# A third of w2 loaded by four 32-row transfers that only eight of the sixteen DMA engines carry

## The chip, the cores and the metric

The kernel runs on one core of a Trainium2 chip. The metric is the device time of one execution in microseconds. All runs quoted are in the fast state, except the single run of e4, whose state is unknown; the profile is of one such execution, and its span is about 2 us shorter than the time. In the profile, DVE is VectorE, PE is TensorE (PEld its weight loads), ACT is ScalarE, and SP issues loads. "Engine" without such a name means one of the sixteen DMA engines.

## The reference, cut to what matters

```python
# x (4, 1, 640), 32 heads of 192, K and V caches (4, 32, 8192, 192), window W = 2048, all bf16
xn = layernorm(x)
q = (xn @ wq), by head
p = softmax(q . k_window * 192 ** -0.5);  o = p . v_window
attention = o @ wo                                   # wo (6144, 640)
h = silu(xn @ w1) * (xn @ w3)                        # w1, w3 (640, 1536)
ffn = h @ w2                                         # w2 (1536, 640)
return x + attention + ffn
```

It is a decode step: four tokens against 201 MB of K and V. Everything is read once, 223 MB in all.

## The kernel before

K and V of a head are one transfer of 3 MB each, 128 partitions by 24,576 bytes; two K tiles and three V tiles are in memory at a time. DVE multiplies K by q, TensorE adds over the head size, a chain of small instructions makes the softmax, TensorE takes P times V. All loads but a first small one of x come from one queue, SP's, in program order. The feed-forward part is spread between the heads; its last weight, w2, comes at the very end.

```python
def ffn_h():                       # h, and its 32x32 transposes, so that 128 of the 1536 rows lie on 128 partitions
    nc.vector.tensor_tensor(out=hb[:].rearrange("p c r -> p r c"),
                            in0=ffn.pop("ps")[:].rearrange("p (r c) -> p r c", c=FC),
                            in1=sT[:].rearrange("p (r c) -> p r c", c=FC), op=ALU.mult)
    nc.vector.transpose(out=hT[:].rearrange("p c r -> p (c r)"), in_=hb[:].rearrange("p c r -> p (c r)"))

w2_v = B_w2.rearrange("(p c) n -> p c n", c=FC)      # FC = 12 columns of rows on 128 partitions
W2C = [0, FC - 4, FC - 2, FC]                        # three pieces: 8, 2 and 2 columns

def w2_load(i):
    if i == 0:
        ffn["w2"] = fpool.tile([P, FC, D], BF16, tag="w", name="w2")
    c0, c1 = W2C[i:i + 2]
    nc.sync.dma_start(out=ffn["w2"][:, c0:c1, :].rearrange("p c n -> p (c n)"),
                      in_=w2_v[:, c0:c1, :].rearrange("p c n -> p (c n)"))

def ffn_out(i):
    for c in range(*W2C[i:i + 2]):
        acc_add(hT[:, c, 0:B], ffn["w2"][:, c, :], last=(c == FC - 1))
# ... (cut)
for h in range(H - 2, H):                            # the order of the last loads, behind the last K tile
    add(NU - 6, 0, load_v, h, 1 + (h == H - 1))
add(NU - 6, 0, w2_load, 0)
add(NU - 6, 0, wo_load, NG - 2)
add(NU - 6, 0, wo_load, NG - 1)
add(NU - 6, 0, w2_load, 1)
add(NU - 6, 0, w2_load, 2)
add(e - 1, 8, ffn_out, 0)
add(e - 1, 8, ge_proj, NG - 2, 0, RPP)               # ge_proj: the attention output times wo
add(e, 6, ge_proj, NG - 1, 0, RPP)
add(e, 7, ffn_out, 1)
add(e, 7, ffn_out, 2)
```

Of the kernel before, what the change touches and what calls it, by code (L numbers as in the profile page):

```python
# [12 lines left out]
ALU = mybir.AluOpType  # L13
# [5 lines left out]
def kernel(  # L19
# [20 lines left out]
    nc = tc.nc  # L40
# [6 lines left out]
    FC = F // P  # L47
# [8 lines left out]
    CT = 32  # L56
    QW = HG * Dh
    RPP = QW // P
    NU = H * GQ
# [54 lines left out]
    for k0 in range(0, KC, 2):  # L114
        n = min(2, KC - k0)
        wt = vpool.tile([P, 2, H * Dh], BF16, tag="vt")
        nc.sync.dma_start(out=wt[:, 0:n, :].rearrange("p k n -> p (k n)"),
                          in_=wq_v[:, k0:k0 + n, :].rearrange("p k n -> p (k n)"))
# [83 lines left out]
    def acc_add(lhsT, rhs, last=False):  # L202
        for i in range(2):
            acc_half(i, lhsT, rhs, last=last)
# [120 lines left out]
    sT = const.tile([P, FW], FP32, name="sT")  # L325
    hb = const.tile([P, FC, CT], BF16, name="hb")
    hT = const.tile([P, FC, CT], BF16, name="hT")
    ffn = {}
# [14 lines left out]
        nc.scalar.activation(out=sT[:], in_=ffn.pop("ps")[:], func=ACTF.Silu)  # L343

    def ffn_h():
        nc.vector.tensor_tensor(out=hb[:].rearrange("p c r -> p r c"),
                                in0=ffn.pop("ps")[:].rearrange("p (r c) -> p r c", c=FC),
                                in1=sT[:].rearrange("p (r c) -> p r c", c=FC), op=ALU.mult)
        nc.vector.transpose(out=hT[:].rearrange("p c r -> p (c r)"), in_=hb[:].rearrange("p c r -> p (c r)"))

    w2_v = B_w2.rearrange("(p c) n -> p c n", c=FC)
    W2C = [0, FC - 4, FC - 2, FC]

    def w2_load(i):
        if i == 0:
            ffn["w2"] = fpool.tile([P, FC, D], BF16, tag="w", name="w2")
        c0, c1 = W2C[i:i + 2]
        nc.sync.dma_start(out=ffn["w2"][:, c0:c1, :].rearrange("p c n -> p (c n)"),
                          in_=w2_v[:, c0:c1, :].rearrange("p c n -> p (c n)"))
# [4 lines that stand above are left out]
# [3 lines left out]
    def add(slot, phase, fn, *args):  # L367
        sched[slot].append((phase, len(sched[slot]), fn, args))
# [31 lines left out]
    e = ends[H - 1][1] + 1  # L400
    for hg in range(NG - 2):
        a = ((hg + 1) * HG - 1) * GQ + L + 3
# [7 lines left out]
    add(f + 8, 0, ffn_load, "w3", B_w3)  # L410
    add(f + 15, 7, ffn_in, "w3")
    add(f + 15, 9, ffn_h)
    add(8, 0, x_load)
    add(16, 6, x_add, 0)
    add(17, 6, x_add, 1)


    for h in range(H - 2, H):
        add(NU - 6, 0, load_v, h, 1 + (h == H - 1))
    add(NU - 6, 0, w2_load, 0)  # L420
    add(NU - 6, 0, wo_load, NG - 2)
    add(NU - 6, 0, wo_load, NG - 1)
    add(NU - 6, 0, w2_load, 1)
    add(NU - 6, 0, w2_load, 2)
    add(e - 1, 8, ffn_out, 0)
    add(e - 1, 8, ge_proj, NG - 2, 0, RPP)
    add(e, 6, ge_proj, NG - 1, 0, RPP)
    add(e, 7, ffn_out, 1)
    add(e, 7, ffn_out, 2)

    for s in sorted(sched):
        for phase, _, fn, args in sorted(sched[s], key=lambda e: (e[0], e[1])):
# [38 lines left out]
```

## Time and profile before

| | before |
|---|---|
| time, median of 3 runs | 529.59 us (529.48 to 531.6) |
| span of the profiled run | 527.6 us |
| moved | 223.31 MB, 423 GB/s |
| DVE, PE busy | 65%, 67% |
| last K tile landed, by its sixteen completion records | 498.62 us |
| last piece of w2 landed | 523.85 us |
| last instruction (copy of the result) starts | 524.62 us |

The lines of this profile stand in the prediction below. Two more things of the trace are used throughout. *Completion records*: a 128-partition transfer leaves sixteen, the small reload of x four, each of the change's new transfers eight (with fewer than sixteen the trace has one more at the issue, which is not counted here). They are taken as one from each engine that carried the transfer, as it is done, so the spread of the sixteen tells how far apart the engines run. *Packet records*: size, start and duration of every packet, without the engine's number. Undisturbed, a packet of 24,576 bytes takes 0.912 us, of 12,288 bytes 0.460, of 7,680 bytes 0.291 and of 2,560 bytes 0.102; in the kernels with 5,120-byte rows, an undisturbed row takes 0.196.

### The profile page before, as it was taken

The page shows a single profiled execution, that of the slowest core. Times are in us where ns is not written, and L with a number is a line of the kernel's source. Part 1 is how long each engine was busy: PE and PEld are TensorE (multiplying, and loading weights), DVE is VectorE, ACT ScalarE, POOL GpSimd, SP SyncE. Part 2 cuts the span into 40 slices and gives each one's busy share as a digit, 9 for nine tenths or more (in the row PEclk, how much of TensorE's full clock was granted, in tenths as well). Part 3 has the DMA queues.
Part 4 walks back from the last instruction along what each step waited for, and adds up shares of the span by engine and source line. Part 5 has one row for each costly group of instructions (what it writes and reads, how often), then busy time and mean ns, then how long its engine had stood idle before and what let it go on. Part 6 is the DMA issues. An engine that isn't in the chain of part 4 may idle for free.

```text
span 527.6 us, 5428 instructions
## 1 busy us (share of the span) xinstructions
PE 353.5 (67%) x2306; PEld 142.6 (27%) x2307; DVE 345.6 (65%) x435; ACT 45.6 (9%) x143; POOL 1.1 (0%) x8
## 2 busy tenths in 40 slices
PE   2865886765657476577637866577566777675686
PEld 0322332322212232223212322223222332232233
DVE  3179775776458567686637876577657867677661
ACT  2111000100211000000000000000000000000010
POOL 0000000000000000000000000000000000000000
PEclk9889887899878989789997998789997988799788
DMA  8999999999999999999999999999999999999994
GB/s 358 434 430 415 420 439 434 430 434 419 439 438 427 432 427 437 429 434 428 432 432 432 432 427 435 432 432 430 432 430 432 432 430 434 429 435 427 438 419 203
DMA packets 11719, 223.31 MB, mean 423 GB/s; under 512 B 1312, under 2 KB 1328, under 8 KB 2608
## 3 DMA queue, kind: packets, MB, share of 16 engines
q1 hardware_dynamic: 11680, 222.97, 98.6%
q8 instruction: 18, 0.29, 0.2%
q14 instruction: 5, 0.04, 0.0%
q10 hardware_dynamic: 16, 0.01, 0.0%
HBM read 222.96 MB, written 0.01 MB: 423 GB/s over the span
## 4 chain that ended last, share of the span: by engine, by line
DMA 57%; DVE 22%; PE 18%; ACT 2%; issue 1%; SPq 0%
DMA kt<-in_A_k_cache_dram 54%; DVE pr L219 15%; PE ps L230 9%; PE po L307 4%; DVE sc L238 3%; DMA wt<-in_A_wq_dram 3%; PE qps L179 2%; PE o_ps L282 2%; DVE z L274 1%; ACT ex L266 1%; PE mt L260 1%; DVE oT L315 1%; DVE og L312 0%; PE acc L200 0%; ACT L266 0%
## 5 line engine op out<-in xcount | busy, mean ns | idle before, releaser
L230 PE MATMUL ps<-pr,idb 128*128 128x512 bf16 x768 | 208.5, 412 | 152.3 <-DVE pr L219 152.3
L219 DVE TENSOR_TENSOR pr<-kt,qbc 128x3072 bf16<-128x3072 bf16 x128 | 223.5, 1746 | 113.9 <-DMA kt<-in_A_k_cache_dram 113.9
L230 PEld LDWEIGHTS <-idb 128*128 128x128 bf16 x768 | 74.4, 102 | 258.7 <-issue 200.1
L238 DVE TENSOR_REDUCE sc<-ps 128x16 f32<-128x512 f32 x128 | 87.2, 681 | 2.0 <-PE ps L230 2.0
L282 PE MATMUL o_ps<-vt,z 128*8 128x384 bf16 x1024 | 60.6, 373 | 2.7 <-DMA vt<-in_A_v_cache_dram 2.7
L307 PE MATMUL po<-o_sb,sel_w 128*32 128x192 f32 x128 | 49.1, 517 | 1.1 <-ACT o_sb L289 1.1
L282 PEld LDWEIGHTS <-z 128*8 128x8 bf16 x1024 | 26.2, 94 | 32.8 <-issue 22.8
L289 ACT COPY o_sb<-o_ps 128x384 f32<-128x384 f32 x32 | 15.3, 479 | 189.7 <-PE o_ps L282 189.7
L274 DVE TENSOR_TENSOR z<-ex,mask_b 128x256 bf16<-128x256 bf16 x32 | 13.5, 422 | 22.0 <-ACT ex L266 22.0
L263 ACT COPY negm<-mt 128x1 f32<-128x1 f32 x32 | 5.1, 159 | 259.0 <-PE mt L260 259.0
L307 PEld LDWEIGHTS po<-o_sb,sel_w 128*32 128x32 f32 x128 | 13.6, 128 | 26.8 <-issue 25.0
L179 PE MATMUL qps<-wt,xnT 128*128 128x512 bf16 x59 | 17.2, 456 | 4.8 <-DMA wt<-in_A_wq_dram 4.7
L185 DVE CAST qbc<-qps 128x512 bf16<-128x512 f32 x6 | 3.8, 684 | 18.7 <-PE qps L179 18.7
L260 PEld LDWEIGHTS mt<-ones_ff,gneg 1*128 1x128 f32 x64 | 9.5, 186 | 13.8 <-issue 11.7
L252 DVE TENSOR_REDUCE gmax<-mt 1x4 f32<-1x128 f32 x32 | 8.8, 275 | 6.6 <-PE mt L247 6.6
L260 PE MATMUL mt<-ones_ff,gneg 1*128 1x1 f32 x64 | 12.2, 258 | 0.0
L247 PE MATMUL mt<-idf,lmax 128*1 128x128 f32 x32 | 10.6, 330 | 1.1 <-DVE lmax L242 1.1
L266 ACT ACTIVATE ex<-sc,negm 128x64 bf16<-128x64 f32 x32 | 11.1, 348 | 1.0
L179 PEld LDWEIGHTS <-xnT 128*128 128x128 bf16 x60 | 6.7, 112 | 14.8 <-issue 9.7
L200 PE MATMUL acc<-wo_t,oT 128*4 128x320 bf16 x96 | 9.2, 298 | 0.4 <-DVE oT L315 0.4
L294 PEld LDWEIGHTS po<-rsum,tot_w 128*32 128x32 f32 x64 | 4.6, 110 | 14.1 <-issue 12.5
L242 DVE TENSOR_REDUCE lmax<-sc 128x1 f32<-128x64 f32 x32 | 7.0, 220 | 1.1
(52 smaller groups left out, 64.2 us busy)
## 6 DMA issues: line engine op xcount, KB each, us to landing
kt<-in_A_k_cache_dram SPq DMA_DIRECT2D x32, 3072.0 KB, 19.0
vt<-in_A_v_cache_dram SPq DMA_DIRECT2D x31, 3072.0 KB, 26.1
wo_t<-in_A_wo_dram SPq DMA_DIRECT2D x8, 960.0 KB, 20.5
wt<-in_A_wq_dram SPq DMA_DIRECT2D x2, 3072.0 KB, 13.3
w<-in_B_w_dram SPq DMA_DIRECT2D x2, 1920.0 KB, 27.1
vt<-in_A_v_cache_dram SPq DMA_DIRECT2D x2, 1536.0 KB, 31.2
wt<-in_A_wq_dram SPq DMA_DIRECT2D x1, 1536.0 KB
w<-in_B_w_dram SPq DMA_DIRECT2D x1, 1280.0 KB, 33.6
```

Source lines behind the costliest of these rows:

```text
L179: nc.tensor.matmul(qp[:], lhsT=xnT[:, kc].rearrange("p a b -> p (a b)"), rhs=wq_rows[kc][:, (c0 + i) * QC:(c0 + i + 1) * QC], start=(kc == ...
L200: nc.tensor.matmul(acc[i * CT:i * CT + B, :], lhsT=lhsT, rhs=rhs[:, i * N0:(i + 1) * N0], start=first, stop=last)
L219: nc.vector.tensor_tensor(out=pr[:], in0=kts[h][:, g * JQ:(g + 1) * JQ, :], in1=qbc[:, h * Dh:(h + 1) * Dh].unsqueeze(1).to_broadcast([P, ...
L230: nc.tensor.matmul(ps[:], lhsT=idb[:], rhs=pr[:, :, kk * DD:(kk + 1) * DD], start=(kk == 0), stop=(kk == NK - 1))
L238: nc.vector.tensor_reduce(out=scs[h][:, g * JQ:(g + 1) * JQ], in_=pss.pop(u)[:], axis=AX.X, op=ALU.add)
L247: nc.tensor.transpose(out=mt[0:1, 0:P], in_=chs[h][0][:], identity=idf[:])
L260: nc.tensor.matmul(mt[:, P:P + 1], lhsT=gneg[:].rearrange("o p b -> o (p b)"), rhs=ones_ff[0:1, 0:1], start=True, stop=True)
L266: nc.scalar.activation(out=ex[:], in_=scs.pop(h)[:], func=ACTF.Exp, bias=negm[:, 0:1], scale=SCALE, accum_out=rsum[:])
L274: nc.vector.tensor_tensor(out=z[:], in0=ex[:].unsqueeze(2).to_broadcast([P, NJ, B]), in1=mask_b[:].unsqueeze(1).to_broadcast([P, NJ, B]), ...
L282: nc.tensor.matmul(o_ps[c * CT:c * CT + 2 * B, :], lhsT=z[:, 2 * jj:2 * jj + 2, :], rhs=vt[:, 2 * jj:2 * jj + 2, :], start=(jj < 4), stop= ...
L289: nc.scalar.copy(out=o_sb[:], in_=o_ps[:])
L307: nc.tensor.matmul(po[sl, 0:Dh], lhsT=sel_w[:, par].rearrange("p a b -> p (a b)"), rhs=o_sb[:, par * Dh:(par + 1) * Dh].rearrange("p (r i) ...
```

## The change

The last transfers end on one half of the engines 2 to 3 us before the other half (the last piece of w2: seven records at 519.27 to 520.03 us, eight at 521.77 to 522.58, one at 523.85). The change gives a third of w2 (columns 0 to 3 of 12, 655 kB) to eight engines alone, so that the others have less to do. To confine it to eight, the 32 rows are named in HBM as 8 by 4 (each of the four new transfers left eight records), and h is permuted to match by four small multiplies. The third is also moved ahead of the last two V tiles, right behind the last K tile.

```diff
--- before.py
+++ after.py
@@ -343,17 +343,27 @@
         nc.scalar.activation(out=sT[:], in_=ffn.pop("ps")[:], func=ACTF.Silu)
 
     def ffn_h():
-        nc.vector.tensor_tensor(out=hb[:].rearrange("p c r -> p r c"),
-                                in0=ffn.pop("ps")[:].rearrange("p (r c) -> p r c", c=FC),
-                                in1=sT[:].rearrange("p (r c) -> p r c", c=FC), op=ALU.mult)
+        ps = ffn.pop("ps")
+        nc.vector.tensor_tensor(out=hb[:, WB:FC, :].rearrange("p c r -> p r c"),
+                                in0=ps[:].rearrange("p (r c) -> p r c", c=FC)[:, :, WB:FC],
+                                in1=sT[:].rearrange("p (r c) -> p r c", c=FC)[:, :, WB:FC], op=ALU.mult)
+        for a in range(CT // 8):
+            nc.vector.tensor_tensor(out=hb[:, 0:WB, a:CT:CT // 8].rearrange("p c r -> p r c"),
+                                    in0=ps[:].rearrange("p (r c) -> p r c", c=FC)[:, a * 8:a * 8 + 8, 0:WB],
+                                    in1=sT[:].rearrange("p (r c) -> p r c", c=FC)[:, a * 8:a * 8 + 8, 0:WB], op=ALU.mult)
         nc.vector.transpose(out=hT[:].rearrange("p c r -> p (c r)"), in_=hb[:].rearrange("p c r -> p (c r)"))
 
     w2_v = B_w2.rearrange("(p c) n -> p c n", c=FC)
-    W2C = [0, FC - 4, FC - 2, FC]
+    WB = 4
+    W2C = [0, WB, FC - 4, FC - 2, FC]
 
     def w2_load(i):
         if i == 0:
             ffn["w2"] = fpool.tile([P, FC, D], BF16, tag="w", name="w2")
+            for w in range(HG):
+                nc.sync.dma_start(out=ffn["w2"][w * CT:(w + 1) * CT, 0:WB, :].rearrange("p c n -> p (c n)"),
+                                  in_=w2_v[w * CT:(w + 1) * CT, 0:WB, :].rearrange("(a e) c n -> e a (c n)", e=8))
+            return
         c0, c1 = W2C[i:i + 2]
         nc.sync.dma_start(out=ffn["w2"][:, c0:c1, :].rearrange("p c n -> p (c n)"),
                           in_=w2_v[:, c0:c1, :].rearrange("p c n -> p (c n)"))
@@ -415,18 +425,20 @@
     add(17, 6, x_add, 1)
 
 
+    add(NU - 6, 0, w2_load, 0)
     for h in range(H - 2, H):
         add(NU - 6, 0, load_v, h, 1 + (h == H - 1))
-    add(NU - 6, 0, w2_load, 0)
+    add(NU - 6, 0, w2_load, 1)
     add(NU - 6, 0, wo_load, NG - 2)
     add(NU - 6, 0, wo_load, NG - 1)
-    add(NU - 6, 0, w2_load, 1)
     add(NU - 6, 0, w2_load, 2)
+    add(NU - 6, 0, w2_load, 3)
     add(e - 1, 8, ffn_out, 0)
+    add(e - 1, 8, ffn_out, 1)
     add(e - 1, 8, ge_proj, NG - 2, 0, RPP)
     add(e, 6, ge_proj, NG - 1, 0, RPP)
-    add(e, 7, ffn_out, 1)
     add(e, 7, ffn_out, 2)
+    add(e, 7, ffn_out, 3)
 
     for s in sorted(sched):
         for phase, _, fn, args in sorted(sched[s], key=lambda e: (e[0], e[1])):
```

## The prediction

In the prediction, and in what was expected of the runs, the engines that carry the new transfers are called the *lower* eight, the rest the *upper* eight. The trace does not number engines; that the four of x are among the lower, and that those are the ones that run ahead, were my assumptions. *Port conflict* is my name for a loss that I supposed where lower engines write partitions 64 to 127 while upper ones have packets in flight. That two engines would then get half the speed each was my estimate, from no trace.

> **What bounds the kernel now.** I read the page first (engine shares, the 40 slices, the queues, the chain by engine), then the chain in order of time for the last 48 us, then the timeline of that stretch, then a table of one-microsecond windows for the last transfers, and at last the completion records of each transfer (one per DMA engine, sixteen per transfer).
>
> The page: the DMA row of the 40 slices, the chain by engine, and the queues.
>
> ```profile
> DMA  8999999999999999999999999999999999999994
> ...
> DMA 57%; DVE 22%; PE 18%; ACT 2%; issue 1%; SPq 0%
> ...
> q1 hardware_dynamic: 11680, 222.97, 98.6%
> q8 instruction: 18, 0.29, 0.2%
> q14 instruction: 5, 0.04, 0.0%
> ```
>
> The transfers run at their full rate until the last slice: 38 of 40 slices show 9. The kernel streams 223 MB, and the chain is DMA, with short pieces of DVE and PE between. Besides the data queue there are 18 packets of instructions on q8 (16,384 bytes each) and a few on q14. They look like nothing; the argument needs them below.
>
> The chain in order of time, end of the kernel (start us, us, what):
>
> ```profile
> 479.88 18.75 DMA kt<-in_A_k_cache_dram
> 498.62 0.02 issue
> 498.64 1.77 DVE pr L219
> ...
> 513.89 2.69 PE o_ps L282 x32
> ...
> 520.03 0.49 ACT o_sb L289
> ...
> 522.16 0.43 DVE og L312
> 522.62 0.39 DVE oT L315
> 523.01 0.04 issue
> 523.05 1.54 PE acc L200 x20
> 524.59 0.02 issue
> 524.62 0.48 DVE res L437
> ```
>
> The last transfer on the chain is the last K tile (head 31), landed at 498.62. After it come 26.0 us of compute (524.62 − 498.64) with no DMA in it, then the output. So the V tiles, w2 and wo that land after 498.62 matter only if one comes later than its reader gets to it. The closest is at the very end, in the timeline:
>
> ```profile
> 523.05 0.98 PE L200 MATMUL acc<-wo_t,oT 128*4 128x320 bf16 x12 [0.40 <-DVE oT L315]
> 523.73 0.50 PEld L200 LDWEIGHTS <-hT 128*4 128x4 bf16 x8
> 523.86 0.71 PE L200 MATMUL acc<-w,hT 128*4 128x320 bf16 x8
> ```
>
> The last two pieces of w2 landed at 523.00 and 523.85 by the completion records. The eight matmuls on them start at 523.86, straight after the twelve on wo (one per 0.068 us); the four on the last piece start about 524.13. So the slack of the last piece is some 0.25 us. The other readers have more: the second half of the last V tile landed at 514.64, read after 518; the first w2 piece at 517.68, read at 520.58; the last wo at 522.24, read at 523.05.
>
> Windows (us, PE, PEld, DVE, ACT, POOL, clock, DMA share, GB/s) where the transfers run out:
>
> ```profile
> 518.00:519.00 1.00, 1.00 (x20) 0.40 (x16) 0.17 (x1) 0.00 (x0) 0.00 (x0) 1.00 0.99 405
> 519.00:520.00 1.00, 0.99 (x17) 0.35 (x8) 0.00 (x0) 0.00 (x0) 0.00 (x0) 1.00 0.68 284
> 520.00:521.00 1.00, 0.44 (x10) 0.38 (x13) 0.00 (x0) 0.48 (x1) 0.00 (x0) 1.00 0.53 213
> 521.00:522.00 1.00, 1.00 (x24) 0.71 (x18) 0.00 (x0) 0.00 (x0) 0.00 (x0) 1.00 0.49 195
> 522.00:523.00 1.00, 0.65 (x11) 0.20 (x6) 0.80 (x2) 0.00 (x0) 0.00 (x0) 1.00 0.13 45
> ```
>
> For over 2 us only half of the engines still work. The completion records of the last piece say the same: seven engines at 519.27 to 520.03, eight at 521.77 to 522.58, one at 523.85. That is what the change is after. The cause fits the instruction packets: after each q8 packet one engine is about 1.45 us further behind in the next landings; the first eight packets (49 to 243 us) make eight engines late once, the next eight (271 to 471 us) late twice (2.9 us), and the one at 505.5 makes one late a third time. The five q14 packets cost one other engine 0.5 us each, 2.5 us. The last K tile shows it too: seven engines at 495.43 to 496.20, nine at 497.95 to 498.62.
>
> **Is the late half the upper half?** The trace does not number engines, but the small reload of x (4 rows) completed on four engines only, at 67.90, 67.92, 68.03 and 68.64. At that time one engine was 0.5 us late (q14's) and one 1.4 us (q8's first). The offsets fit one q14 engine among the four and no q8 engine. So I take q8's eight to be the upper eight, q14's one of the lower: about 85%.
>
> [...] In the trace each engine moves 24,576 bytes in 0.912 us, 26.9 GB/s[...].
>
> **The change part by part.**
> 1. *ffn_h.* One DVE multiply of 384 columns (1.86 us at 174.7) becomes one of 256 and four of 32. With 0.17 us fixed (the shortest DVE instruction, the reciprocal at 518.72), 4.4 ns a column: 1.29 + 4 × 0.31 = 2.5 us, so +0.7 us of DVE, once. In the stretch from 165 to 185 us DVE waits 7.0 us for K tiles; the K issues run 18 us ahead of landing. On the path: 0.
> 2. *PE.* The same 24 matmuls on hT in the same two places. 0.
> 3. *Issues.* Three more on the SP queue, about 0.55 us each as V's. The eight completion semaphores are reused in turn, so the third w2 piece now waits for the K tile at 498.62 and the later ones for the new transfers (about 499 to 503). At that time 7 us of V or more are queued on each engine. On the path: 0.
> 4. *Bytes.* The first third is 655 KB. Per lower engine 16 rows of 5,120 bytes; a row about 0.197 us (between 0.102 for 2,560 and 0.291 for 7,680): 3.2 us. Before, two thirds took each engine 8 × 0.385 = 3.1 us; now the second third takes 8 × 0.197 = 1.6. So the lower engines get 4.8 (+1.7), the upper 1.6 (−1.5). The last landing by this: upper 520.3 to 521.1, one at 522.3; lower 520.9 to 521.7, and q14's engine at 521.9 + 1.7 = 523.6. From 523.85 to about 523.6: not a gain, as PE came there at 524.13.
> 5. *Place.* The third goes in the queue right behind the last K tile, ahead of V. V31 then lands around 515.8 for 514.64: still ahead of 518. 0.
> 6. *Ports.* [...] The leading lower engines finish K31 at 495.4 to 495.8, do the first two transfers in 1.6 us, and from about 497.0 to 497.4 [...] the upper engine loses what it had left, 1.2 to 1.5 us, and K31 lands at about 499.9. That is the landing on the chain: +1.3 us, all of it on the path.
>
> Sum: 0 without step 6, +1.3 us with it.
>
> **Rivals.** (a) *Balance only*: no port conflict; 529.6. For it: an engine's own rate may be the limit. (b) *Port conflict*: 530.9. [...] (c) *The tail was bound by the last w2 landing and shrinks*: 523.85 and 523.86 look like it, and would give up to −1 us; against it, the chain's twelve wo matmuls end just there. 529.0. (d) *The late engines are not the upper ones*: then a late one gets +1.7 us, the last w2 lands at about 525.5, 1.1 us over the slack: 530.7. I hold (b) 50%, (a) 30%, (c) 8%, (d) 12%.
>
> **Range and chances.** Weighted: 0.5 × 530.9 + 0.3 × 529.6 + 0.08 × 529.0 + 0.12 × 530.7 = 530.3 us. The before runs spread from 529.48 to 531.6, so 529.2 to 531.6. Two per cent is 10.6 us; nothing here makes a fifth of it: within 2% at 98%, faster and slower 1% each.
>
> **What would show it.** Right: sixteen rows of 5,120 bytes on eight engines; DMA share falling from full to none within about 1.5 us at the end; K31 landing late by 1.3 us against the tile before it, with packets twice their length around 497 to 500 (b), or not (a). Wrong: a V or w2 landing on the chain, a wait of DVE at 175 us that delays a K issue, or a chain of compute after K31 not 26 us long.

## The result, and the profile after

| | before | after |
|---|---|---|
| median of 4 runs | 529.54 us (529.41 to 531.6) | 533.05 us (532.4 to 534.01) |
| ratio of fast runs | | 1.0059, 95% interval 1.003 to 1.0088 |
| span of the profile | 527.6 us | 530.5 us |
| last V tile but two, last K tile landed | 491.34, 498.62 us | 491.29, 500.08 us |
| last piece of w2 landed | 523.85 us | 527.07 us |
| copy of the result starts | 524.62 us | 527.59 us |

A ratio is the mean time of one kernel's fast runs over that of the other's of the same rounds, so not quite the ratio of the medians quoted. The change made the kernel 0.6% slower, inside the 2% that the verdict calls the same, and outside the predicted range.

First the rates in the 40 slices. Before:

```profile
GB/s 358 434 430 415 420 439 434 430 434 419 439 438 427 432 427 437 429 434 428 432 432 432 432 427 435 432 432 430 432 430 432 432 430 434 429 435 427 438 419 203
```

After, with its DMA row and its chain by engine:

```profile
DMA  8999999999999999999999999999999999999995
GB/s 358 437 423 413 426 443 430 429 441 426 426 437 432 424 432 440 427 430 439 430 424 435 431 425 434 435 431 434 430 429 432 429 435 435 426 437 426 344 404 217
...
DMA 61%; DVE 20%; PE 15%; ACT 2%; issue 1%; SPq 1%
```

The DMA row hides what the GB/s row shows: slices 38 and 39 moved 344 and 404 GB/s, for 438 and 419 before, with the engines at 9 of 10 throughout. A slow packet counts as a busy engine: from 500 to 505 us the share is 0.97 at 268 GB/s. The table of windows has both in one line (us, busy time of PE, PEld, DVE, ACT, POOL, clock, DMA share, GB/s). Before:

```profile
495.00:500.00 5.00, 1.81 (x6) 0.63 (x6) 2.29 (x3) 0.00 (x0) 0.00 (x0) 0.63 1.02 437
500.00:505.00 5.00, 4.49 (x15) 1.86 (x15) 4.47 (x8) 0.01 (x1) 0.00 (x0) 0.68 0.98 420
```

After:

```profile
495.00:500.00 5.00, 1.91 (x6) 0.68 (x6) 0.93 (x2) 0.00 (x0) 0.00 (x0) 0.62 1.04 311
500.00:505.00 5.00, 3.08 (x8) 1.14 (x8) 4.36 (x5) 0.00 (x0) 0.00 (x0) 0.50 0.97 268
```

In these 10 us the share is the same and the bytes fall by a third. By the packet records, between 496.8 and 508.0 us 63 packets of 24,576 bytes took over 1.2 times their undisturbed 0.912 us, up to 1.89, and 71 of the new rows over 1.2 times their 0.196, up to 0.416. Summed over 485 to 526 us, the new rows lost 12.3 us of engine time and the others 40.2 us: 52.5 us, or 3.3 us for each of sixteen engines. Before lost 0.5 us in all, in the one packet that followed an instruction packet (0.914 us for 0.460); the 40.2 hold one such loss too. The last w2 piece is 3.2 us later.

The timeline of the end, after:

```profile
500.11 1.76 DVE L219 TENSOR_TENSOR pr<-kt,qbc 128x3072 bf16<-128x3072 bf16 x1 [4.17 <-DMA kt<-in_A_k_cache_dram]
...
523.27 0.98 PE L200 MATMUL acc<-wo_t,oT 128*4 128x320 bf16 x12 [0.84 <-DMA wo_t<-in_A_wo_dram]
...
525.55 0.98 PE L200 MATMUL acc<-wo_t,oT 128*4 128x320 bf16 x12 [1.30 <-DMA wo_t<-in_A_wo_dram]
...
526.36 0.44 PE L200 MATMUL acc<-w,hT 128*4 128x320 bf16 x4
527.11 0.44 PE L200 MATMUL acc<-w,hT 128*4 128x320 bf16 x4 [0.31 <-DMA w<-in_B_w_dram]
...
527.59 0.48 DVE L449 CAST res<-acc 36x320 bf16<-36x320 f32 x1 [4.30 <-PE acc L200]
```

The last K tile is 1.5 us late at DVE (500.11 for 498.64). But the last head's normalisation began at 522.47 for 522.16 (part of the 1.5 us is made up, with a higher granted clock in between: P times V of head 30 took 1.47 us at a clock of 1.00, for 2.69 at 0.50). From there PE waits for wo twice and for w2 once. These three waits on transfers were not there before. **The end is now set by the last landings**, not by compute. The two half-idle microseconds did not go away either:

```profile
522.00:523.00 1.00, 0.43 (x6) 0.02 (x1) 0.50 (x2) 0.00 (x0) 0.00 (x0) 1.00 0.79 323
...
524.00:525.00 1.00, 0.25 (x4) 0.03 (x1) 0.00 (x0) 0.00 (x0) 0.00 (x0) 1.00 0.26 108
525.00:526.00 1.00, 0.45 (x8) 0.31 (x9) 0.00 (x0) 0.00 (x0) 0.00 (x0) 1.00 0.21 82
526.00:527.00 1.00, 0.80 (x12) 0.43 (x9) 0.00 (x0) 0.00 (x0) 0.00 (x0) 1.00 0.11 44
```

A quarter of the engines, then a fifth, then a tenth work on alone for over two microseconds. The completion records of the last piece name them: two engines at 521.08 and 521.28, ten from 524.02 to 524.72, one at 525.67, three at 526.72 to 527.07. The new transfers' own records (eight each, as intended) fall into two parts, for the last of them five at 500.20 to 501.25 and three at 504.67 to 505.10. So three of the eight that carry them were late ones.

The hidden layer went as predicted or better:

```profile
174.66 1.28 DVE L347 TENSOR_TENSOR hb<-f_ps,sT 128x256 bf16<-128x256 f32 x1
175.55 0.96 DVE L351 TENSOR_TENSOR hb<-f_ps,sT 128x32 bf16<-128x32 f32 x4
```

The five multiplies are over at 176.51 for 176.54 before (they overlap), and nothing waits for them.

Two suspects are left, and they can act together: the conflict that comes with rows written to partitions 64 to 127 (P), and late engines among the lower eight that get extra bytes (L).

### The profile page after: what moved, and what is told of

Its sections match the earlier page's. It is cut to its first block, busy times and chain, and to the rows that moved or that the text cites. A ratio compares the mean times of both kernels' runs of the same rounds, so it can differ in the third digit from the quotient of the medians.

```text
span 530.5 us, 5438 instructions
## 1 busy us (share of the span) xinstructions
PE 355.0 (67%) x2307; PEld 142.7 (27%) x2307; DVE 345.6 (65%) x439; ACT 45.6 (9%) x143; POOL 1.1 (0%) x8
## 2 busy tenths in 40 slices
DMA packets 11879, 223.31 MB, mean 421 GB/s; under 512 B 1344, under 2 KB 1360, under 8 KB 2896
## 4 chain that ended last, share of the span: by engine, by line
DMA 61%; DVE 20%; PE 15%; ACT 2%; issue 1%; SPq 1%
DMA kt<-in_A_k_cache_dram 50%; DVE pr L219 14%; PE ps L230 8%; DMA w<-in_B_w_dram 8%; DMA wt<-in_A_wq_dram 3%; DVE sc L238 3%; PE po L307 3%; PE qps L179 2%; DVE z L274 1%; ACT ex L266 1%; PE o_ps L282 1%; PE mt L260 1%; ACT L266 0%; DVE oT L315 0%; DVE og L312 0%
## 5 line engine op out<-in xcount | busy, mean ns | idle before, releaser
L230 PE MATMUL ps<-pr,idb 128*128 128x512 bf16 x768 | 210.8, 416 | 151.8 <-DVE pr L219 151.7
L282 PE MATMUL o_ps<-vt,z 128*8 128x384 bf16 x1024 | 59.2, 366 | 2.8 <-DMA vt<-in_A_v_cache_dram 2.8
L282 PEld LDWEIGHTS <-z 128*8 128x8 bf16 x1024 | 25.8, 92 | 32.5 <-issue 22.3
L294 PEld LDWEIGHTS po<-rsum,tot_w 128*32 128x32 f32 x64 | 4.5, 108 | 13.9 <-issue 12.3
```

Source lines behind the costliest of these rows:

```text
L230: nc.tensor.matmul(ps[:], lhsT=idb[:], rhs=pr[:, :, kk * DD:(kk + 1) * DD], start=(kk == 0), stop=(kk == NK - 1))
L282: nc.tensor.matmul(o_ps[c * CT:c * CT + 2 * B, :], lhsT=z[:, 2 * jj:2 * jj + 2, :], rhs=vt[:, 2 * jj:2 * jj + 2, :], start=(jj < 4), stop= ...
```

## The experiments

The columns of this table are from the profiled run of each: engine time lost from 485 to 526 us by the rows of 5,120 bytes and by all other packets (where there are 256 such rows, half of them are the second third of w2; only in e2 do some of these lose time too); the time from the landing of the V tile ahead of the last K tile to that K tile; from that to the last piece of w2.

| run | rows, others lost, us | V to K, us | K to w2, us | median, us | ratio, 95% interval |
|---|---|---|---|---|---|
| before | none, 0.5 | 7.28 | 25.23 | 529.5 | |
| the change | 12.3, 40.2 | 8.79 | 26.99 | 533.05 | 1.0059 (1.003 to 1.0088) |
| e1_order16 | 0, 0.9 | 7.27 | 25.06 | 530.07 | 1.0018 (1.0005 to 1.0031) |
| e2_late8 | 23.5, 28.0 | 7.27 | 28.30 | 533.31 | 1.0077 (1.0065 to 1.0089) |
| e3_ports | 0, 0.5 | 7.29 | 25.15 | 530.33 | 1.0018 (1.0004 to 1.0033) |
| e5_one_hi | 2.3, 10.6 | 8.29 | 25.51 | 531.54 | 1.0036 (1.0021 to 1.0051) |
| e6_one_lo | 1.7, 8.0 | 7.40 | 25.75 | 529.96 | 1.0011 (0.9996 to 1.0026) |
| e7_fetch4 | none, 0.5 | 7.27 | 24.12 | 530.65 | 1.0029 (1.0005 to 1.0054) |
| e8_clean8 | 0, 0.5 | 7.26 | 24.90 | 530.24 | 1.0005 (0.9986 to 1.0025) |
| e9_rows32_16 | 14.9, 30.3 | 9.07 | 26.39 | 533.79 | 1.0068 (1.0041 to 1.0095) |
| e10_order16_again | 0, 1.0 | 7.30 | 25.35 | 529.38 | 0.9999 (0.9978 to 1.0021) |
| e11_change_again | 12.9, 39.5 | 8.57 | 27.17 | 532.26 | 1.005 (1.0028 to 1.0071) |

All results were correct but e3's, which is wrong on purpose. A caution: runs of one kernel scatter by 1 to 2 us. In two profiles that fell on one of the longest runs of their kernel (e3, 531.46 us; e9, 534.49 us; both in the fast state) the whole extra 2 us were there by the second head's first multiply (43.59 and 43.76 us for 41.59), long before anything that was changed. Runs of before scatter as far (531.6, 531.72, 531.88), but no profile shows where those lost it. That is why the table uses intervals within a profile, and why a difference of 0.2% in the medians is not explained.

**e1_order16 and e10_order16_again: the place alone.** The four transfers become one on sixteen engines, and the hidden layer is one multiply again. (The cuts from here on are shortened; each is against the change, or against before where the run starts from that.)

```diff
         if i == 0:
             ffn["w2"] = fpool.tile([P, FC, D], BF16, tag="w", name="w2")
-            for w in range(HG):
-                nc.sync.dma_start(... 32 rows, 8 engines ...)
-            return
         c0, c1 = W2C[i:i + 2]      # now columns 0 to 3 of all 128 partitions
```

> The new order of the loads kept (first third of w2 right behind the last K tile, ahead of V), but as one 128-partition transfer on all sixteen engines, and the hidden layer made in one DVE instruction as before. If place alone costs nothing, as step 5 of the prediction says: last K tile at 498.6 us, last piece of w2 at about 523.9 us, time 529.6 us (ratio 1.000). Rival, the place itself is what costs (V arrives too late behind w2): over 531 us, with a wait of the P*V matmuls on a V tile.

> The first experiment again (new place, one transfer on sixteen engines), because its five runs lay between 529.2 and 531.5 us although its profile showed no loss. If its 0.18% is the place: again about 1.0018. If it is scatter from the start of the run: about 1.000.

No slow rows, the K tile at its usual distance, the last w2 piece at 523.87 us for 523.85. The first set of runs gave 1.0018, the second 0.9999. The place costs nothing that these runs can show.

**e2_late8: the same transfers away from the K tile.**

```diff
-    add(NU - 6, 0, w2_load, 0)
     for h in range(H - 2, H):
         add(NU - 6, 0, load_v, h, 1 + (h == H - 1))
+    add(NU - 6, 0, w2_load, 0)
```

> The four 8-engine transfers kept, moved behind both V tiles to where the old first piece of w2 was, so that they are queued nowhere near the last K tile. Theory P (the loss is the port conflict that delays the last K tile by 1.46 us): the K tile lands at 498.6 again and the time goes back to 529.6-530 us. Theory L (three of the eight lower engines are late ones and get the extra rows on top, so that the last piece of w2 sets the end): the K tile lands at 498.6, but the last piece of w2 lands at 526-527 us all the same and the time stays at 532-533 us.

Theory P in the narrow form that I predicted, a loss through the last K tile, falls. DVE has the K tile after its usual interval, and the time stays at 533.3 us because of the last landing:

```profile
499.18 1.76 DVE L219 TENSOR_TENSOR pr<-kt,qbc 128x3072 bf16<-128x3072 bf16 x1 [2.57 <-DMA kt<-in_A_k_cache_dram]
```

```profile
525.97 0.98 PE L200 MATMUL acc<-wo_t,oT 128*4 128x320 bf16 x12 [1.29 <-DMA wo_t<-in_A_wo_dram]
526.78 0.44 PE L200 MATMUL acc<-w,hT 128*4 128x320 bf16 x4
527.50 0.44 PE L200 MATMUL acc<-w,hT 128*4 128x320 bf16 x4 [0.28 <-DMA w<-in_B_w_dram]
```

But the conflict itself has only moved with the transfers; here it falls on V and wo:

```profile
510.00:515.00 5.00, 3.43 (x17) 1.26 (x16) 2.40 (x6) 0.39 (x1) 0.00 (x0) 1.00 1.00 312
515.00:520.00 5.00, 4.34 (x71) 2.04 (x70) 0.59 (x2) 1.14 (x5) 0.00 (x0) 1.00 1.00 261
```

The loss is 51.5 us of engine time, as in the change, and the time is as in the change. So in these two runs it did not matter which transfer was slowed: 52.5 and 51.5 us were lost, and the medians are 533.05 and 533.31 us.

**e3_ports: the same engines and bytes, other partitions.** The third and fourth transfers write partitions 0 to 63 of a part of the q tile that is no longer read (not in the cut: a memset clears what they leave unwritten in w2).

```diff
+            spare = qbc[0:2 * CT, 0:WB * D].rearrange("p (c n) -> p c n", c=WB)
             for w in range(HG):
-                nc.sync.dma_start(out=ffn["w2"][w * CT:(w + 1) * CT, 0:WB, :]...
+                dst = ffn["w2"][w * CT:(w + 1) * CT, 0:WB, :] if w < 2 else spare[(w - 2) * CT:(w - 1) * CT, :, :]
+                nc.sync.dma_start(out=dst...
```

> Wrong result on purpose: the third and fourth of the 8-engine transfers write partitions 0 to 63 of a region that is no longer read, in place of partitions 64 to 127 of w2 (which are zeroed). Engines, bytes, rows and order as in the change; only the destination half differs. If [...]: rows of 5120 bytes take 0.197 us each and none about 0.40 us, the last K tile lands at 498.6 us (500.08 in the change), the last piece of w2 at about 524.2 to 525.7 us (522.6 plus 1.66, or with the third instruction fetch on top), and the time is 529.6-531 us. If destinations do not matter: 500.1 us, 527 us and 533 us as in the change.

Not one row was slow: all 256 took 0.196 us, and no packet of 24,576 bytes exceeded 0.912. K tile and last w2 are at before's distances. Here the destination half is what costs: 52.5 us of engine time in the change, 0.5 us in e3. The reads from HBM, their order, the four small transfers and the permuted multiplies are those of the change, so none of these is the cause. The three late engines still carried the extra bytes here (they finished last, 5.3 to 5.8 us behind the first two), and the last w2 piece came 25.15 us after the K tile, for 25.23 before. So late engines among the lower eight cost nothing without the conflict; the last landing only stays where it was, in place of coming earlier as balancing was meant to make it.

**e4_map: which engines are late.** Behind each of the last fifteen K tiles a load of n rows, n = 1 to 15.

```diff
+    def probe(h, n):
+        t = small.tile([P, 64], BF16, tag="probe", bufs=3, name="probe")
+        nc.sync.dma_start(out=t[0:n, :], in_=B_w1[0:n, 0:64])
...
             add((h - KBUFS + 1) * GQ, 0, load_k, h)
+        if h >= H - 15:
+            add((h - KBUFS + 1) * GQ, 0, probe, h, h - (H - 16))
```

> The kernel before with a tiny probe load of n rows (n = 1 to 15, one for each of the last 15 heads) queued behind each K tile. [...] Theory L: the probe of 8 rows shows five engines in time and three late ones, the one of 15 rows seven or so in time in all; the first four engines hold one late one (the 0.5 us steps). My prediction had been: one late engine among the lower eight. Time 529.6-530.2 us; the probes carry 15 kB in all.

The probe of n rows left n packets each time, 120 in all. Some of their starts, in us after the first of the same probe:

```
n=3   0.00 0.47 0.69
n=4   0.00 0.47 0.69 1.54
n=5   0.00 0.47 0.47 0.70 1.54
n=7   0.00 0.47 0.47 0.70 2.37 2.63 3.01
n=8   0.00 0.05 0.52 0.52 0.75 2.42 2.68 3.06
n=9   0.00 0.09 0.14 0.61 0.61 0.84 2.51 2.77 3.15
n=15  0.00 0.09 0.14 0.61 0.61 0.84 2.51 2.77 2.85 2.92 2.93 2.93 2.95 2.95 3.15
```

No record gives an engine's number. Here an engine is numbered by the probe that adds it: number n - 1 is the one that the probe of n rows has and that of n - 1 rows has not; that each probe keeps the engines of the one before is my reading of the starts, which largely repeat from line to line. Reading up so, engines 0, 1, 2, 4, 7 and 8 are early; 3, 5, 6 and 9 to 14 are late; with seven early in every K tile, 15 is early. Three of the first eight are late, as three of the eight that carry the new transfers were. With those eight as the lower, the late half is not the upper half. In the one run, 529.41 us, the probes cost nothing that shows.

**e5_one_hi and e6_one_lo: 17 rows on one engine.** To the kernel before, one dummy load of 17 rows, which one engine carries alone (one completion record each). In e5 it writes partitions 64 to 80, in e6 partitions 0 to 16. Theory "pair" has one other packet slow at any moment, theory "wide" more than one.

```diff
+    def one_engine():              # e5: p0 = 64; e6: p0 = 0
+        nc.sync.dma_start(out=qbc[p0:p0+17, 0:4 * D], in_=w2_v[0:17, 0:4, :].rearrange("p c n -> p (c n)"))
...
+    add(NU - 6, 0, one_engine)
     for h in range(H - 2, H):
         add(NU - 6, 0, load_v, h, 1 + (h == H - 1))
```

> The kernel before plus one dummy load of 17 rows of 5120 bytes behind the last K tile, into partitions 64 to 80 of a region that is no longer read (the result stays right). [...] Question: in the change the writers' own rows lost 12.3 us in all, [...] but the other packets lost 40.2 us, over three times that. Theory pair[...]: the 17 rows take about 0.39 us each, at any moment one other packet is slow, the 24,576-byte packets lose about 3.3 us in all. Theory wide[...]: they lose 10 us or more. Time 529.4 to 530.5 us[...].

> The same dummy load of 17 rows into partitions 0 to 16[...]. If the loss comes from crossing from the lower engines to the upper half of the partitions: no slow packet here, all rows 0.197 us. Time 529.4 to 530 us.

The rows took 0.196 us at first, then up to 0.446 us. The others did not behave as pairs. Beside single packets of 1.2 to 1.7 us, nearly every packet of 24,576 bytes in flight took 0.92 to 1.17 us for 0.912. In e5 those packets lost 9.7 us against 2.3 us of the rows, in e6 7.5 against 1.7 (0.5 us of e6's is behind an instruction packet). That is just under the 10 us that I had set for theory "wide" in e5, but about three times the 3.3 us of theory "pair" there, and in e6 about four times the rows' own loss; so more than one other engine is slowed. e6 shows that writing to partitions 64 to 127 is not needed: 17 rows to partitions 0 to 16 lost 1.7 us and the others 7.5. Both wrote into the q tile, as e3's harmless rows do, so the tile is not the cause either. Why the others slow down, no record here shows. e5's time, 531.54 us, was above what I expected: its K tile was 1.0 us later against the V tile, and its first multiply of head 1 was 0.8 us late from the start.

**e7_fetch4: more instruction packets.**

```diff
+    def idle_pe(u):
+        for i in range(4):
+            nc.tensor.matmul(po[0:B, Dh + 1:Dh + 5], lhsT=idb[0:B, 0:B], rhs=idb[0:B, 0:4], start=True, stop=True)
...
             add(u + 1, 2, adder, u)
+            add(u + 1, 2, idle_pe, u)
```

> The kernel before with 512 tiny matmuls added ([...] four more instruction packets of 16 KiB), four per K quarter, beside the adders where PE waits for DVE. If instruction packets make their engines late (1.45 us each): 22 packets in place of 18, four engines late a third time before the last K tile, which lands about 1.4 us later than before (500.0 us in place of 498.6, and 4.6 us behind the leaders in place of 3.2), and the time is 530.5 to 531.5 us. If the late engines are late for another reason: 498.6 us, 3.2 us of spread and 529.5 to 529.9 us[...].

The queue's line in its page, and DVE's wait for the last K tile:

```profile
q8 instruction: 22, 0.36, 0.2%
```

```profile
500.38 1.76 DVE L219 TENSOR_TENSOR pr<-kt,qbc 128x3072 bf16<-128x3072 bf16 x1 [3.57 <-DMA kt<-in_A_k_cache_dram]
```

22 packets for 18, the last K tile at 500.35 us (498.62 before; 0.4 us of this was there by the first multiply of head 1), its last engine 4.71 us behind its first (3.19 before), and 0.29% more time. The evidence is the spread, not the time, since the added matmuls also kept PE busy for 30.4 us. The lateness of the late engines comes from the instruction packets: one more packet on an engine, 1.5 us more.

**e8_clean8: the intent without the conflict, right result.** All four 8-engine transfers go to partitions 0 to 63; the h values of the other half are copied down to match.

```diff
+        nc.vector.tensor_copy(out=hT2[:], in_=hT[2 * CT:4 * CT, 0:WB, :])
...
+            ffn["w2b"] = qbc[0:2 * CT, 0:WB * D].rearrange("p (c n) -> p c n", c=WB)
+                dst = ffn["w2"][w * CT:(w + 1) * CT, 0:WB, :] if w < 2 else ffn["w2b"][(w - 2) * CT:(w - 1) * CT, :, :]
...
+        if i == 0:
+            for c in range(WB):
+                acc_add(hT[0:2 * CT, c, 0:B], ffn["w2"][0:2 * CT, c, :])
+                acc_add(hT2[:, c, 0:B], ffn["w2b"][:, c, :])
+            return
```

> The intent of the change without its conflict and with the right result: the same four 8-engine transfers of 32 rows, all of them into partitions 0 to 63 (the rows of the upper half go to a region of the lower half that is no longer read, their hidden values are copied down once, and the first third takes 16 matmuls of 64 rows in place of 8 of 128, +0.5 us of PE beside the last head's sums). If the port conflict is the whole loss: no slow packet, last K tile 7.3 us after the V tile ahead of it, last piece of w2 25.1 us after the last K tile (27.0 in the change, 25.2 before), time 529.4-530.5 us. If three late lower engines cost by themselves: 26 us or more and over 531 us. A gain over before is not expected on either: three lower engines are late too, and 26 us of compute follow the last K tile.

```profile
495.00:500.00 5.00, 1.91 (x6) 0.68 (x6) 2.35 (x3) 0.00 (x0) 0.00 (x0) 0.64 0.98 418
500.00:505.00 5.00, 4.46 (x15) 1.81 (x15) 4.49 (x8) 0.00 (x0) 0.00 (x0) 0.68 1.04 447
```

Full rate where the change had 311 and 268 GB/s, no slow packet, and a ratio of 1.0005: the loss is gone with the conflict. There is no gain either (the median is 0.7 us above before's). The transfers end where they did (523.60 us), and the 64-row matmuls, which I had put beside the last head's sums, ran after them:

```profile
522.11 0.30 PE L200 MATMUL acc<-w,hT 64*4 64x320 bf16 x2
...
523.83 1.80 PE L200 MATMUL acc<-wo_t,oT 128*4 128x320 bf16 x24
```

That pushed all 24 matmuls on wo behind them and the copy to 526.21 us, so in this profile compute sets the end again.

**e9_rows32_16: 32-row transfers on all sixteen engines.** e1 with the transfer cut into four, rows in their plain order. That sixteen carry each shows in the pages: e9 has 64 packets under 512 bytes more than before (1,376 for 1,312), sixteen for each of the four, and the change 32 (1,344), eight for each.

```diff
+            for w in range(HG):
+                nc.sync.dma_start(out=ffn["w2"][w * CT:(w + 1) * CT, 0:WB, :].rearrange("p c n -> p (c n)"),
+                                  in_=w2_v[w * CT:(w + 1) * CT, 0:WB, :].rearrange("p c n -> p (c n)"))
+            return
```

> Four 32-row transfers again at the same place, but of the plain kind that all sixteen engines carry, two rows each: no choice of engines[...]. If what costs is [...]: rows of 5120 bytes near 0.39 us, the last K tile more than 8 us after the V tile ahead of it, last w2 1.5 us or more later against the K tile, time 531-533 us. If what costs is giving bytes to late engines: as with one 128-partition transfer, 529.3-530 us.

```profile
495.00:500.00 5.00, 2.97 (x12) 1.06 (x10) 3.26 (x4) 0.00 (x0) 0.00 (x0) 0.83 1.08 361
500.00:505.00 5.00, 0.56 (x2) 0.25 (x2) 2.36 (x2) 0.00 (x0) 0.00 (x0) 0.50 0.97 271
```

The same bytes as in e1 on sixteen engines, and the loss is back: 45.2 us of engine time, 0.68% of time. So it is neither the choice of eight engines nor the late ones that costs. What was measured is this. Packets slow (those behind an instruction packet left out) with 8-engine rows of which half go to partitions 64 to 127 (the change and e2, 52.5 and 51.5 us lost), with 17 rows of one engine to 64 to 80 or to 0 to 16 (e5 and e6, 12.9 and 9.7 us) and with 32-row transfers on sixteen engines (e9). With 8-engine rows to partitions 0 to 63 (e3, e8) or one 128-partition transfer (e1), no row was slow and 0.5 to 0.9 us were lost. My explanation, that an engine slows others where it writes partitions that another engine writes in the transfers around it, was not shown: no record tells which engine writes which partitions.

**e11_change_again.**

> The change itself, in the same rounds as the three above, for comparison with them on one chip: 533 us, ratio 1.006 to 1.0075.

1.005, a little under the first measurement, with the same lost engine time and the same distances.

In the runs with a large conflict, the lost time shared among sixteen engines is about the delay of the end of the stream: the change 52.5 / 16 = 3.3 us, with the last w2 3.2 us later; e2 51.5 / 16 = 3.2, with 3.1 (its K tile's 0.5 us taken off); e9 45.2 / 16 = 2.8, with 3.0 (2.2 us taken off, by which its V tile was late before the conflict); e11 52.4 / 16 = 3.3, with 3.2 (0.7 taken off likewise). The small conflicts give 0.6 with 0.6 (e6) and 0.8 with 1.3 (e5).

## Why the prediction was wrong

The step that failed is step 6: a conflict where it expected one was measured, but the cost it gave was too small and it was put on the wrong path. It gave +1.3 us, through the last K tile; the stream lost 52.5 us of engine time, 3.3 us an engine, and the last landing of w2 set the end.

- *Step 6, ports: the size.* The loss came with the transfers to partitions 64 to 127 and went with them (52.5 us in the change, 0.5 in e3 and e8), and the delay of the last K tile was nearly right (+1.46 us for +1.3). That the loss is one between two engines was my estimate, and was not shown. The own rows' loss came as worked out (12.3 us, eight engines by 1.5), but I gave only about the same again to the other engines. The others lost 40.2 us; beside one engine's 17 rows, too, they lost 9.7 us for 2.3 and 7.5 for 1.7 (e5, e6). So "nothing here makes a fifth" of two per cent (2.1 us) was wrong too: the change cost 3.5 us.
- *Step 6, ports: where it lands.* The 26 us of compute after the last K tile were the path before, with 0.25 us of slack for the last w2 piece. I added the K tile's delay to this path and left the last landing at 523.6 us. In fact the transfers took the end over: PE waits 0.84, 1.30 and 0.31 us for wo and w2, and e2, whose K tile is on time, is as slow as the change.
- *Which engines are late.* Also wrong, but not what cost the time. I took q8's eight for the upper eight at 85%; in e4's order they are 5, 6 and 9 to 14. The four records of x hold for four engines only and could not tell more. Late engines did get the extra rows, as rival (d) says, and ended last. But with the same engines and bytes and no conflict, the last w2 piece comes 32.4 (e3) and 32.2 us (e8) after the V tile, for 32.5 before and 35.8 in the change; and e9, which gives the late engines no more than the others, has 35.5.
- *The causes as exclusive rivals.* (b) and (d) got separate shares, though nothing keeps them apart, and their sum was never formed. Made after the result, from the prediction's terms, it is 522.58 for a late lower engine, plus 1.66 for the extra bytes, plus 1.5 for eight rows at double length: 525.7 us for the last w2. It landed at 527.07; the other 1.3 us is loss of that engine's other packets. The records of the last K tile agree: those of all nine late engines, three lower ones among them (e4), moved from the stretch 497.95 to 498.62 us to the stretch 499.08 to 500.08 us, where the prediction had only upper ones delayed. Rival (d) itself has a slip: 525.5 is 1.4 us after PE's 524.13, not 1.1.
- *The range.* It is the scatter of before's runs, not moved by what each rival adds. Rival (b) with that scatter reaches about 533, but by scatter, not by what happened. The 98% for "within 2%" held.
- *Steps 1, 2 and 3* held: DVE's extra work is hidden, PE has the same matmuls, no wait came from an issue (there are four more issues, not three; the trace has landings on eight semaphores, and the second third of w2 waited 8.2 us for the K tile's, to be issued at 500.10 us, the later ones 0.6 to 1.3 us each for the new transfers'). *Step 5* held for the place (e10), but under the conflict the second half of the last V tile landed at 519.43 us, not 515.8, and PE went on with it at 519.47 after a stop of 0.3 us.
- *Lateness from instruction packets, 1.45 us each,* held (e7: 4.71 us of spread for 3.19).
- *Rival (a)*, balance without conflict, is what e8 built: 1.0005. *Rival (c)* had no support: even without a conflict nothing was gained at the end.

**Left open:** why the other engines slow down; which engine writes which partitions; whether the 0.18% of e1 and e3 is only scatter (e10 suggests so for e1; e3 was not repeated); and which engines an instruction queue uses in another program.

## What to carry to other kernels

When engines that move data side by side finish apart, first find out which ones are late (a probe of n rows per transfer did it here, at no cost that one run showed), and then ask where the bytes land: in these runs the same rows from eight engines lost nothing in partitions 0 to 63 (e3, e8) and 12.3 us with half of them in 64 to 127, and rows that lost time cost the others more than themselves: 40.2 us for the 12.3 in the change, 30.3 for 14.9 in e9, 9.7 for 2.3 in e5, 7.5 for 1.7 in e6. Read GB/s beside the DMA share: here a share of 0.97 at 268 GB/s, for 0.98 at 420 before, was a conflict. And when causes can act together, work out their sum too: two small risks to the same landing add up, and a slack of 0.25 us covers neither.
